# One engine for the fourth sorted pair, a gate before the next loads, two unread products fewer, and expert 0's w2 in two transfers

## The chip, the cores and the metric

The kernel runs on one core of a Trainium2 chip. The metric is the device time of one execution in microseconds (us). In the profile, PE is TensorE (products), PEld its weight loads, DVE is VectorE, ACT is ScalarE, POOL is GpSimd and SP is SyncE. POOL and SP also issue DMA transfers. Times inside an execution are counted from the start of its span.

## What is computed

Two stages follow each other. The first is an attention with sorted blocks: for 4 batches and 8 heads, a sequence of 768 rows of 64 is cut into 8 blocks of 96. A small 8x8 matrix per head is normalised five times by rows and columns and then mixes the blocks of keys and of values:

```python
k_sorted = np.einsum('bhij,bhjcd->bhicd', P, k_b)
v_sorted = np.einsum('bhij,bhjcd->bhicd', P, v_b)
scores = scale * np.matmul(q_b, k_sb.transpose(0, 1, 2, 4, 3))
out = np.matmul(softmax(scores), v_sb)
```

The second stage is a mixture of 8 experts over the resulting 3072 rows of 512: routing weights from a gate, normalised eight times, and for each expert `relu(x @ w1[e]) @ w2[e]` with w1 of 512x1024 and w2 of 1024x512, summed with the routing weights.

## The kernel before

The work is one long program for the five engines. What each engine does is in the order of its queue; most products and all POOL transfers are pinned to the order in which the program was written (`pin`), the other instructions are placed by the framework's scheduler, which also sets all semaphores. The first 38 us hold batch 0 and the start of batch 1. From 38 to about 92 us the attention of batches 1 to 3 is woven with expert 0's products for the batches already done, and then experts 1 to 7 follow for the rest of the time.

**Loads.** All loads from memory that convert to bf16 are issued by POOL, in this order (lines 91 to 97, then 476, 477 and 501, 502): q, v and k of batch 0 in halves of four heads; the gate's weights; the first half of expert 0's w1 (512 KB); later, after the hop of batch 0, the second half of w1 (`load_w1`, L82), v of batch 1 (`load_batch`, L72), the product R for batch 1 (`build_r`, L135, two POOL multiplications), k and two q loads of batch 1, and w2 of expert 0 (`load_w2`, L88, one transfer of 1024 KB). v and k of batch 2 come behind that; q of batch 2 waits for a free buffer.

**Sorting the values of batch 0** (`sort_pair`, L267 to 279, called for the four pairs of heads hp = 0 to 3). Two products (L271) fill a PSUM pair, and one engine copies it into the tile `vs`: ACT for pairs 0 and 2, DVE for pair 1. Pair 3 is shared: DVE copies the first head, ACT the second.

**The hop** (`hop`, L148 to 153). The sorted values must change partitions, so eight transfers of 97.5 KB move `vs` to `vsb`, one for each block: pieces 0, 2, 4, 6 are issued by SP and 1, 3, 5, 7 by POOL.

**Keys, scores, mixes.** `wide_keys` (L294 to 306, "k") makes the sorted keys of a pair of heads; ACT copies those of pair 0 and DVE those of pairs 1 to 3. `half_scores` (L308 to 322, "s") does four of the eight blocks for one pair of heads and ACT takes the exponential. `half_mix` (L328 to 343, "m") multiplies by the sorted values that the hop brought: m00 to m03 read pieces 0 to 3, m10 to m13 pieces 4 to 7. `half_turn` ("t") transposes the result, `half_hidden` ("h") does expert 0's first product (h02 and h03 read the second half of w1), and "v" sorts the values of batch 1 with `sort_pair`. "p" spreads the 8x8 matrices for R. `output0` (L398 to 407) reads w2 in its eight parts, the first four in a first step.

**Unread products** (`warm`, L324 to 326) are products of a blank tile that nobody reads. A table says how many stand ahead of a step. The order of all of this is written out by hand in lines 471 to 503:

```python
unread = {"s03": 1, "s10": 1, "s11": 1, "s12": 1, "m00": 3, "m02": 1, "m03": 1,
          "m10": 1, "m11": 1}
for x in ("s00 k2 s01 k3 p s02 s03 s10 s11 s12 m00 s13 m01 m02 m03 t00 m10 m11 t01 h00 "
          "m12 m13 h01 t10 h02 v0 t11 v1 h03 v2 v3 h10").split():
```

Of two digits the first is the half of the blocks (for "h" and "t" too) and the second the pair of heads or the group; one digit is the pair of heads. The PSUM pairs have four buffers, so a step also waits until the copy of an earlier step has freed one.

Of the kernel before, what the change touches and what calls it, by code (L numbers as in the profile page):

```python
# [20 lines left out]
def mkap(t, dims, off=0):  # L21
    return bass.AP(tensor=t.tensor, offset=t.offset + off, ap=dims)
# [3 lines left out]
def kernel(  # L26
# [11 lines left out]
    nc = tc.nc  # L38
    B, H, S, D = 4, 8, 768, 64
    NB, BL = 8, 96  # L40
    N, Dm, E, F = 3072, 512, 8, 1024
# [22 lines left out]
    pin = tc.keep_in_program_order  # L64
    kt, vt, qt = {}, {}, {}

    def load_batch(bb, parts):
        for x, l0, n in parts:
            d, src = {"v": (vt, v), "k": (kt, k), "q": (qt, q)}[x]
            if bb not in d:  # L70
                d[bb] = kvp.tile([128, 8, 384], BF16, name="kvq", bufs=5)
            pin(nc.gpsimd.dma_start(  # L72
                out=d[bb][:, l0:l0 + n, :],
                in_=src[bb, l0:l0 + n].rearrange("h (p kk) d -> p h (kk d)", kk=6)))

    w1t = {}
    w2t = {}

    def load_w1(e, f0=0, f1=F):
        if e not in w1t:  # L80
            w1t[e] = wp.tile([128, 4, F], BF16, name="w1e")
        pin(nc.gpsimd.dma_start(  # L82
            out=w1t[e][:, :, f0:f1],
            in_=moe_w1[e].rearrange("(kk k) f -> k kk f", k=128)[:, :, f0:f1]))

    def load_w2(e):
        w2t[e] = (wq if e else wcp).tile([128, 8, Dm], BF16, name="w2e")
        pin(nc.gpsimd.dma_start(out=w2t[e],  # L88
                                in_=moe_w2[e].rearrange("(fb k) f -> k fb f", k=128)))

    load_batch(0, [("q", l0, 4) for l0 in (0, 4)])
    Ibig = ones.tile([128, 128], BF16)
# [11 lines left out]
    VW = NB * 520  # L104
    vsbt = [perp.tile([128, VW], BF16, name=f"vsb{n}") for n in range(2)]
    vs = vsp.tile([128, 6, 8, 65], BF16)
# [145 lines left out]
    held = pp.tile([96, 2], BF16)  # L252
# [14 lines left out]
    def sort_pair(bb, hp, pair):  # L267
        t = pair()
        warm(t, bb == 0 and hp == 0)
        for h in range(2):  # L270
            pin(nc.tensor.matmul(t[:, h, 0:384], Rt[bb][:, 2 * hp + h].rearrange("p i c -> p (i c)"),  # L271
                                 vt[bb][:, 2 * hp + h, :], start=True, stop=True))
        shared = bb == 0 and hp == 3
        for eng, h0, h1 in (((nc.vector.tensor_copy, 0, 1), (nc.scalar.copy, 1, 2)) if shared else
                            ((nc.vector.tensor_copy if hp % 2 else nc.scalar.copy, 0, 2),)):
            ins = eng(vs[:, :, 2 * hp + h0:2 * hp + h1, 0:64],
                      t[:, h0:h1, 0:384].rearrange("p h (kk d) -> p kk h d", d=64))
            if shared:
                pin(ins)

    def wide_queries(hp, pair):
        qT[0, hp] = sp.tile([128, 128, 6], BF16, name="qTs", bufs=4)
        t = pair()
        for kk in range(6):
            for h in range(2):
                c = (kk % 3) * 128
                pin(nc.tensor.matmul(t[64 * h:64 * h + 64, kk // 3, c:c + 128],
                                     qt[0][:, 2 * hp + h, kk * 64:kk * 64 + 64], Ibig,
                                     start=True, stop=True))
        pin(nc.scalar.copy(  # L290
            qT[0, hp].rearrange("p x (b j) -> p x b j", b=2),
            t[:, :, 0:384].rearrange("p b (j x) -> p x b j", j=3)))

    def wide_keys(hp, pair):  # L294
        kT[0, hp] = sp.tile([128, NB, 16, 6], BF16, name="kTs", bufs=4)
        t = pair()
        for kk in range(6):
            for h in range(2):
                c = (kk % 3) * 128
                pin(nc.tensor.matmul(t[64 * h:64 * h + 64, kk // 3, c:c + 128],  # L300
                                     kt[0][:, 2 * hp + h, kk * 64:kk * 64 + 64],
                                     Rt[0][:, 2 * hp + h].rearrange("p i c -> p (i c)"),
                                     start=True, stop=True))
        pin((nc.vector.tensor_copy if hp else nc.scalar.copy)(
            kT[0, hp].rearrange("p i c (b j) -> p (i c) b j", b=2),
            t[:, :, 0:384].rearrange("p b (j x) -> p x b j", j=3)))
# [17 lines left out]
    def warm(t, n):  # L324
        for _ in range(n):
            pin(nc.tensor.matmul(t[:, 0, :], blank[:, 0:128], blank, start=True, stop=True))
# [102 lines left out]
    with tc.tile_pool(name="ps0", bufs=4, space=bass.MemoryType.PSUM,  # L429
                      reuse_waits="tile") as ps0:  # L430
        pair = lambda: ps0.tile([128, 2, 512], F32, name="pair")
        warm(pair(), 11)
        rs = pp.tile([32, 8], F32)
        cs = pp.tile([32, 8], F32)
        Pt = P.rearrange("p i j -> p j i")
        nc.vector.reduce_max(out=rs, in_=P, axis=AX.X)
        nc.vector.tensor_sub(P, P, mkap(rs, [rs.ap[0], rs.ap[1], [0, 8]]))
        for it in range(5):


            pin(nc.scalar.activation(out=P, in_=P, func=AF.Exp))
            if it == 3:
                warm(pair(), 3)
            for hp in {2: (0, 1), 3: (2,), 4: (3,)}.get(it, ()):
                wide_queries(hp, pair)
            if it == 1:
                pin(nc.vector.reduce_sum(out=mask16, in_=Ibig.rearrange("p (j c) -> p c j", c=16),
                                         axis=AX.X))
            pin(nc.vector.reduce_sum(out=rs, in_=P, axis=AX.X))
            nc.vector.reciprocal(out=rs, in_=rs)  # L450
            nc.vector.tensor_mul(P, P, mkap(rs, [rs.ap[0], rs.ap[1], [0, 8]]))
            nc.vector.reduce_sum(out=cs, in_=Pt, axis=AX.X)
            if it == 0:
                nc.vector.tensor_scalar_add(cs, cs, 1e-9)
            nc.vector.reciprocal(out=cs, in_=cs)
            nc.vector.tensor_mul(Pt, Pt, mkap(cs, [cs.ap[0], cs.ap[1], [0, 8]]))

        Prep = perp.tile([32, 8, 8, 16], BF16, name="R1")
        for eng, i0, n in ((nc.vector.tensor_copy, 0, 5), (nc.scalar.copy, 5, 3)):
            eng(Prep[:, i0:i0 + n], mkap(P, [P.ap[0], [8, n], [1, 8], [0, 16]], off=i0 * 8))  # L460

        def spread(n):
            t = pair()
            warm(t, n)
            pbps = t[:, 0, 0:256].rearrange("p (i g) -> p i g", i=8)
            for i in range(8):
                pin(nc.tensor.matmul(pbps[:, i, :], Prep[:, i].rearrange("p j c -> p (j c)"),
                                     Ibig[0:32, 0:32], start=True, stop=True))
            return pbps

        build_r(0, nc.vector, 2, spread(13))
        for hp in range(4):
            sort_pair(0, hp, pair)
        wide_keys(0, pair)
        hop(0)
        load_w1(0, 512, F)
        load_batch(1, [("v", 0, 8)])
        wide_keys(1, pair)
        halves = [mps.tile([128, 8, 384], BF16, name="hTs") for _ in range(2)]
        unread = {"s03": 1, "s10": 1, "s11": 1, "s12": 1, "m00": 3, "m02": 1, "m03": 1,  # L480
                  "m10": 1, "m11": 1}
        for x in ("s00 k2 s01 k3 p s02 s03 s10 s11 s12 m00 s13 m01 m02 m03 t00 m10 m11 t01 h00 "
                  "m12 m13 h01 t10 h02 v0 t11 v1 h03 v2 v3 h10").split():
            n = [int(c) for c in x[1:]]
            if x[0] == "s":
                half_scores(*n, pair, unread.get(x, 0))
            elif x[0] == "m":
                half_mix(*n, pair, unread.get(x, 0))
            elif x[0] == "t":
                half_turn(*n, lambda: ps0.tile([128, 2048], BF16, name="pair"),  # L490
                          nc.vector.tensor_copy if x == "t11" else nc.scalar.copy)
            elif x[0] == "h":
                half_hidden(*n, halves[n[0]], pair)
            elif x[0] == "v":
                sort_pair(1, *n, pair)
            elif x[0] == "k":
                wide_keys(*n, pair)
            else:
                nc.vector.tensor_copy(Pb, spread(0).rearrange("p i g -> p g i"))
                build_r(1, nc.gpsimd, 4)  # L500
                load_batch(1, [("k", 0, 8), ("q", 0, 4), ("q", 4, 4)])
                load_w2(0)
        hop(1)
# [323 lines left out]
    for n in range(1, 3 * (E - 1) + 1):  # L827
        e, p, hT = 1 + (n - 1) // 3, (n - 1) % 3, hTs[n - 1]
        d = 2 + n // 3
# [49 lines left out]
```

## Time and profile before

| what | value |
|---|---|
| median of 3 runs | 676.18 us (675.96 to 676.72) |
| the profiled execution | 677.16 us |
| its span, first to last instruction | 675.2 us |
| granted TensorE clock | 1.000 |
| DMA packets | 32671, 36.57 MB, mean 54 GB/s |
| PE busy, 24 to 26 us / 26 to 28 us / 28 to 30 us | 2.00 / 0.65 / 1.77 of 2 us |
| DMA, 20 to 22 / 22 to 24 / 28 to 30 / 34 to 36 us | 178 / 136 / 201 / 203 GB/s |
| POOL idle before its q load at 37.27 us | 9.6 us |

The span is what the profile's rows cover; the profiled execution's own time is 1.96 us longer. A row of the timeline gives the start, the length, the engine, the line of the program, the operation, what it writes and reads, and how many instructions are merged in it; a bracket at its end tells how long the engine was idle before it and what ended that wait. A row of the waits gives who waited for whom, the total, how often, and the longest. A DMA row gives the transfer, the queue that issued it, how many, the size of each, and the median time from issue to landing.

### The profile page before, as it was taken

The page shows a single profiled execution, that of the slowest core. Times are in us where ns is not written, and L with a number is a line of the kernel's source. Part 1 is how long each engine was busy: PE and PEld are TensorE (multiplying, and loading weights), DVE is VectorE, ACT ScalarE, POOL GpSimd, SP SyncE. Part 2 cuts the span into 40 slices and gives each one's busy share as a digit, 9 for nine tenths or more (in the row PEclk, how much of TensorE's full clock was granted, in tenths as well). Part 3 has the DMA queues.
Part 4 walks back from the last instruction along what each step waited for, and adds up shares of the span by engine and source line. Part 5 has one row for each costly group of instructions (what it writes and reads, how often), then busy time and mean ns, then how long its engine had stood idle before and what let it go on. Part 6 is the DMA issues. An engine that isn't in the chain of part 4 may idle for free.

```text
span 675.2 us, 13291 instructions
## 1 busy us (share of the span) xinstructions
PE 661.3 (98%) x5155; PEld 435.8 (65%) x5155; DVE 544.0 (81%) x1135; ACT 295.7 (44%) x530; POOL 470.2 (70%) x494
## 2 busy tenths in 40 slices
PE   7899999999999999999999999999999999999996
PEld 3666676554666666666666666666666666666675
DVE  6548777663798888888898888888898888888896
ACT  4673863479433333333434343333434343333430
POOL 4612445007987998898897998689886999636745
PEclk9999999999999999999999999999999999999999
DMA  9997964002140340031203040034003120001223
GB/s 158 184 220 121 151 113 64 1 0 40 24 64 2 63 62 1 1 63 17 48 1 62 2 64 1 2 62 63 1 1 64 19 46 1 1 1 63 94 78 142
DMA packets 32671, 36.57 MB, mean 54 GB/s; under 512 B 2016, under 2 KB 25696, under 8 KB 32608
## 3 DMA queue, kind: packets, MB, share of 16 engines
q0 software_dynamic: 26720, 27.42, 25.9%
q1 hardware_dynamic: 5888, 8.30, 3.7%
q8 instruction: 40, 0.66, 0.4%
q14 instruction: 23, 0.19, 0.1%
HBM read 52.45 MB, written 6.29 MB: 87 GB/s over the span
## 4 chain that ended last, share of the span: by engine, by line
PE 73%; DVE 1%; POOL 1%; issue 0%; ACT 0%; DVEq 0%
PE oacc L736 36%; PE bk L649 36%; PE bk L736 1%; DVE osbl L701 1%; POOL hs L719 1%; DVE hT L685 0%; DVE hT L688 0%; ACT p L669 0%; DVEq L701 0%
## 5 line engine op out<-in xcount | busy, mean ns | idle before, releaser
L701 DVE SCALAR_TENSOR_TENSOR osbl<-oacc,glog,osbl 128x256 f32<-128x256 f32 (+1 forms) x490 | 255.3, 521 | 61.5 <-PE oacc L736 61.3
L649 PE MATMUL bk<-xtT,w1e 128*128 128x512 bf16 x504 | 149.7, 379 | 0.0
L719 POOL TENSOR_TENSOR hs<-hT 128x512 bf16<-128x512 bf16 (+2 forms) x105 | 99.4, 959 | 67.8 <-DVE hT L688 67.6
L736 PEld LDWEIGHTS <-hs 128*128 128x128 bf16 x1008 | 98.5, 98 | 64.7 <-POOL hs L719 1.5
L736 PEld LDWEIGHTS <-hT 128*128 128x128 bf16 x1008 | 98.6, 98 | 64.5 <-issue 1.3
L736 PE MATMUL oacc<-w2e,hT 128*128 128x256 bf16 x796 | 119.6, 273 | 0.5 <-ACT hT L691 0.5
L691 ACT ACTIVATE hT<-bk 128x512 bf16<-128x512 f32 x84 | 50.3, 598 | 158.5 <-PE bk L649 156.5
L719 POOL TENSOR_TENSOR hs<-hT,hs 128x512 bf16<-128x512 bf16 (+2 forms) x105 | 99.8, 958 | 4.9
L719 POOL TENSOR_TENSOR hs<-hs,hT 128x512 bf16<-128x512 bf16 (+2 forms) x105 | 99.9, 959 | 4.3 <-ACT hT L691 0.4
L649 PE MATMUL bk<-xc,wc 128*128 128x512 bf16 x336 | 99.9, 379 | 0.2 <-ACT p L669 0.2
L736 PE MATMUL oacc<-w2e,hs 128*128 128x256 bf16 x612 | 92.0, 273 | 0.9 <-POOL hs L719 0.9
L677 ACT COPY u<-bk 128x512 f32<-128x512 f32 x84 | 49.2, 586 | 95.2 <-PE bk L649 94.5
L649 PEld LDWEIGHTS <-w1e 128*128 128x128 bf16 x672 | 65.7, 98 | 10.5
L685 DVE CUSTOM_DVE_ANT_0 hT<-bk,p 128x512 bf16<-128x512 f32 x84 | 58.1, 692 | 11.8 <-ACT p L682 6.4
L695 DVE SCALAR_TENSOR_TENSOR h<-bk,hT 128x512 bf16<-128x512 f32 x84 | 57.2, 681 | 5.8 <-ACT hT L691 5.8
L682 ACT COPY p<-bk 128x512 f32<-128x512 f32 x84 | 49.3, 586 | 23.5 <-PE bk L649 23.5
L669 ACT COPY p<-bk 128x512 f32<-128x512 f32 x84 | 49.3, 587 | 20.3 <-PE bk L649 20.3
L673 DVE CUSTOM_DVE_ANT_0 hT<-bk,p 128x512 bf16<-128x512 f32 x84 | 57.1, 680 | 1.1 <-ACT hT L395 0.6
L688 DVE CUSTOM_DVE_ANT_0 hT<-bk,u 128x512 bf16<-128x512 f32 x84 | 57.1, 679 | 1.0 <-PE bk L649 1.0
L736 PE MATMUL oacc<-w2s,hs 128*128 128x256 bf16 x364 | 54.8, 273 | 0.1
L649 PEld LDWEIGHTS <-wc 128*128 128x128 bf16 x504 | 49.3, 98 | 8.0 <-issue 0.4
L649 PE MATMUL bk<-xtT,wc 128*128 128x512 bf16 x168 | 50.0, 379 | 0.0
(141 smaller groups left out, 838.1 us busy)
## 6 DMA issues: line engine op xcount, KB each, us to landing
w2e<-in_moe_w_dram POOLq DMA_DIRECT2D x8, 1024.0 KB, 8.8
w1e<-in_moe_w_dram POOLq DMA_DIRECT2D x7, 1024.0 KB, 8.1
out_dram<-osbl SPq DMA_DIRECT2D x23, 256.0 KB, 2.0
kvq<-in_v_dram POOLq DMA_DIRECT2D x3, 768.0 KB, 13.1
kvq<-in_k_dram POOLq DMA_DIRECT2D x3, 768.0 KB, 14.0
vsb<-vs SPq DMA_DIRECT2D x20, 97.5 KB, 5.4
kvq<-in_q_dram POOLq DMA_DIRECT2D x4, 384.0 KB, 10.5
kvq<-in_q_dram POOLq DMA_DIRECT2D x2, 768.0 KB, 18.3
```

The source lines that it names most:

```text
L649: hold(nc.tensor.matmul(ps, wa[:, kk, :], xa[:, kk, :], start=(first and kk == 0), stop=(kk == 1), skip_group_check=True))
L669: nc.scalar.copy(p1, u)
L673: nc.vector._custom_dve(TENSOR_ADD_SAT, out=c11, in0=w, in1=p1, s0=TOP, s1=0.0)
L677: nc.scalar.copy(u2, u)
L682: nc.scalar.copy(p5, v)
L685: nc.vector._custom_dve(TENSOR_ADD_SAT, out=c22, in0=u, in1=p5, s0=TOP, s1=0.0)
L688: nc.vector._custom_dve(TENSOR_ADD_SAT, out=c12, in0=v, in1=u2, s0=TOP, s1=0.0)
L691: nc.scalar.activation(out=c21, in_=u, func=AF.Relu)
L695: nc.vector.scalar_tensor_tensor(out=h3[e, p][:, i, :], in0=u, scalar=0.0, in1=c22, op0=ALU.max, op1=ALU.subtract)
L701: nc.vector.scalar_tensor_tensor(out=o, in0=ps, scalar=glog[:, t, e:e + 1], in1=o, op0=ALU.mult, op1=ALU.add)
L719: nc.gpsimd.tensor_tensor(out=c, in0=a, in1=b, op=o)
L736: nc.tensor.matmul(ps, h[:, fb, :], w[:, fb, :], start=(first and fb == 0), stop=(fb == 3), skip_group_check=True)
```

## The change

The shared copy of pair 3 becomes a DVE copy of both heads, as for pair 1, and is no longer pinned. A POOL copy of two columns of `vsb`, the last elements of pieces 0 and 2, is placed behind the hop; the second half of w1 and v of batch 1 are issued behind that copy, and so is all that POOL does later. One unread product each goes from s12 and from m00. The w2 of expert 0 is loaded by two transfers, parts 0 to 3 and 4 to 7; the other experts' w2 stay one transfer.

```diff
     def load_w2(e):
         w2t[e] = (wq if e else wcp).tile([128, 8, Dm], BF16, name="w2e")
-        pin(nc.gpsimd.dma_start(out=w2t[e],
-                                in_=moe_w2[e].rearrange("(fb k) f -> k fb f", k=128)))
+        for f0, f1 in ((0, 8),) if e else ((0, 4), (4, 8)):
+            pin(nc.gpsimd.dma_start(
+                out=w2t[e][:, f0:f1],
+                in_=moe_w2[e].rearrange("(fb k) f -> k fb f", k=128)[:, f0:f1]))
...
-        shared = bb == 0 and hp == 3
-        for eng, h0, h1 in (((nc.vector.tensor_copy, 0, 1), (nc.scalar.copy, 1, 2)) if shared else
-                            ((nc.vector.tensor_copy if hp % 2 else nc.scalar.copy, 0, 2),)):
-            ins = eng(vs[:, :, 2 * hp + h0:2 * hp + h1, 0:64],
-                      t[:, h0:h1, 0:384].rearrange("p h (kk d) -> p kk h d", d=64))
-            if shared:
-                pin(ins)
+        (nc.vector.tensor_copy if hp % 2 else nc.scalar.copy)(
+            vs[:, :, 2 * hp:2 * hp + 2, 0:64],
+            t[:, :, 0:384].rearrange("p h (kk d) -> p kk h d", d=64))
...
         hop(0)
-        load_w1(0, 512, F)
-        load_batch(1, [("v", 0, 8)])
+        gate = nc.gpsimd.tensor_copy(
+            held, mkap(vsbt[0], [[VW, 96], [1040, 2]], off=519))
+        with tc.issue_after(gate.ins):
+            load_w1(0, 512, F)
+            load_batch(1, [("v", 0, 8)])
         wide_keys(1, pair)
         halves = [mps.tile([128, 8, 384], BF16, name="hTs") for _ in range(2)]
-        unread = {"s03": 1, "s10": 1, "s11": 1, "s12": 1, "m00": 3, "m02": 1, "m03": 1,
+        unread = {"s03": 1, "s10": 1, "s11": 1, "m00": 2, "m02": 1, "m03": 1,
                   "m10": 1, "m11": 1}
```

## The prediction

> **What bounds the kernel now.** I read the summary of engines first, then the chain that ended last, then the waits of the first 40 us, and last the timelines of each engine and the DMA issues of that stretch one by one, because everything that the change touches lies between 14 and 50 us of the span.
>
> ```profile
> PE 661.3 (98%) x5155; PEld 435.8 (65%) x5155; DVE 544.0 (81%) x1135; ACT 295.7 (44%) x530; POOL 470.2 (70%) x494
> PE 73%; DVE 1%; POOL 1%; issue 0%; ACT 0%; DVEq 0%
> ```
>
> TensorE works or is queued nearly all the time and carries the chain, so time is won only where TensorE stands still or does work that nobody reads. The waits between 12 and 40 us name the places:
>
> ```profile
> engine line waited for: us in total, times, longest us
> ...
> PE pair L335 <- DMA vsb<-vs: 1.4, 1, 1.4
> ...
> PE pair L315 <- ACT kTs L304: 0.9, 1, 0.9
> ...
> ACT vs L276 <- DVE vs L276: 0.3, 1, 0.3
> ```
>
> TensorE waits once for a hop transfer and once for the first key copy on ACT, and ACT itself waits for DVE inside the shared copy. The ACT timeline shows the second (start, us, engine, line):
>
> ```profile
> 14.22 1.51 ACT L276 CAST vs<-pair 128x768 bf16<-128x768 f32 x2 [1.44 <-PE pair L271]
> 16.01 0.50 ACT L276 CAST vs<-pair 128x384 bf16<-128x384 f32 x1 [0.28 <-DVE vs L276]
> 16.40 0.80 ACT L304 CAST kTs<-pair 128x768 bf16<-128x768 f32 x1
> ```
>
> ACT is done with pairs 0 and 2 at 15.73, waits for DVE's half of pair 3, copies its own half, and only then the first keys. TensorE's timeline shows the first:
>
> ```profile
> 22.21 0.82 PE L326 MATMUL pair<-blank 128*128 128x512 bf16 x3
> 22.87 0.51 PE L335 MATMUL pair<-vsb,atp 96*96 96x65 bf16 x8
> ...
> 25.69 0.33 PE L335 MATMUL pair<-vsb,atp 96*96 96x65 bf16 x4
> 27.37 0.33 PE L335 MATMUL pair<-vsb,atp 96*96 96x65 bf16 x4 [1.35 <-DMA vsb<-vs]
> ```
>
> The mix m00 runs at 22.87 behind three unread products and waits for nothing; m10 does its blocks 4 and 5 at 25.69 and then stands idle from 26.02 to 27.37 for piece 6. POOL and the DMA issues (of 19.5 to 20 us; last column: us to landing) show what shares the DMA engines with that piece:
>
> ```profile
> 16.80 2.11 POOL L151 DMA_DIRECT2D vsb<-vs  x4 [8.88 <-ACT vs L276]
> 18.88 0.82 POOL L82 DMA_DIRECT2D w1e<-in_moe_w_dram  x1
> 19.66 0.94 POOL L72 DMA_DIRECT2D kvq<-in_v_dram  x1
> ```
>
> ```profile
> kvq<-in_v_dram POOLq DMA_DIRECT2D x1, 768.0 KB, 13.1
> w1e<-in_moe_w_dram POOLq DMA_DIRECT2D x1, 512.0 KB, 10.0
> vsb<-vs SPq DMA_DIRECT2D x1, 97.5 KB, 8.3
> ```
>
> SP's pieces 0, 2, 4, 6 go out at 16.54, 17.27, 17.90 and 19.07 and take 3.7, 4.8, 5.9 and 8.3 us: they land at 20.2, 22.1, 23.8 and 27.4. POOL's pieces 1, 3, 5, 7 land at 20.1, 21.1, 21.8 and 22.6. The hop of batch 3 (85.8 to 93.1 us), with no load beside it, takes 3.2, 3.7, 4.6 and 5.3 us for the same four SP pieces. So the loads issued at 18.88 and 19.66 are the likely cause of piece 6's extra 3 us.
>
> **Fourth pair by one engine.** DVE's half (0.547) becomes a whole copy (0.954 in its own rows). DVE is free of pair 1 at 15.43 and then ends pair 3 at 16.39, where ACT ended the shared copy at 16.51: the hop starts 0.12 earlier. DVE's next copy, the keys of pair 1, needs products that end at 16.32 and starts at 16.40 instead of 16.35. ACT skips its wait and its half: its key copy starts when the products are done, 15.75 instead of 16.40, minus 0.65. The scores s00 follow at 16.60 (17.25), k2 at 16.91 (17.56). From there the key copies on DVE set the pace: pair 1 ends 17.35, pair 2 runs 17.50 to 18.41, pair 3 18.41 to 19.32, so s03 starts at 19.37 instead of 20.01. I take minus 0.64. The exponentials on ACT shift as much and stay ahead of their mixes.
>
> **Fewer unread products.** s12 loses one and m00 one. The timeline has 13 of them in 2.98 us, and from 21.58 to 21.90 one costs 0.21 net of overlap: minus 0.43. They kept TensorE busy in a time in which it would have waited, so this counts only if what follows is ready: m00 at 22.87 - 0.64 - 0.43 = 21.80 needs pieces 0 to 3. They landed by 22.1; the earlier start and no load beside them put the last at 21.0 to 22.0. If they stay at 22.1 - 0.12, the loss is 0.2.
>
> **The gate.** A POOL copy of 96x2 that waits for pieces 0 and 2. The trace has a copy of that form at L814: 0.17 us; 0.10 (POOL's memset of 128x1) and 1.0 (its copies of 128x768 at L179) bound it, and I take 0.17, the same shape. Behind it on POOL stand the second half of w1 (18.88), v of batch 1 (19.66), the two R products (20.57), k, q, q, w2 and v, k of batch 2 (22.59 to 27.66). The gate opens when piece 2 lands: at best 17.15 + 3.7 = 20.9 (the hop of batch 3), at worst 22.0; I take 21.2, so the loads begin at 21.5, 2.6 later than now. What it gives: no load runs beside the last pieces. At the pace of the unloaded hop of batch 2 (first issue 62.66, last landing 70.4, 7.7 us) piece 6 lands at 24.2, and m10 asks for it at 27.37 - 1.35 - 1.07 = 24.95. The stall of 1.35 goes. The bounds are 1.35 and nothing (piece 6 as late as now); a loss is excluded, since no transfer is added beside that piece.
>
> What it costs: the loads are queued in order, 203 GB/s when full. A 1024 KB w1 load alone takes 8.1 us, of which 5.2 is transfer at 203 GB/s, so 512 KB takes 5.5: landing 27.0 (28.9 now), needed by h02 at 30.1. v of batch 1 follows 3.9 later, at 30.9; by the row of batch 3's v (7.5 us alone, 3.6 above its transfer) at 31.5. Now it lands at 19.66 + 13.1 = 32.8 and is read at 33.79; with 2.42 gained it is wanted at 31.37. That is what is late next: between 0 and 0.15 lost at 31.5, up to 1.0 if the gate opens at 22.0. I take 0.15.
>
> The R products end at 25.4 and are read at 31.4. k of batch 1 lands 3.9 after v, at 35.1, wanted at 36.5. q, w2, v, k, q follow in a full queue about 1.5 earlier than now while TensorE is 2.3 earlier; their present slacks (k 2.2, first q 3.9, w2 1.7, v of batch 2 some 6, its q 4.8 through the copies on POOL) cover 0.8.
>
> [...]
>
> **w2 in two transfers.** One more issue: two of 0.79 (the row of a 512 KB w1 half) for one of 0.92, plus 0.66 on POOL, hidden in POOL's idle 9.6 us before 37.27; without that cover the loads behind would be 0.66 later. Bounds 0.6 (384 KB issues, 0.75) to 0.9. The first half lands some 2.6 earlier, but w2 as a whole lands now at 47.4 and is read at 49.1; shifted, it is about 45.9 against 46.8. I cost it at nothing; at most it saves a wait should the loads come later than I think.
>
> **The sum.** 0.64 + 0.43 + 1.35 = 2.42, minus 0.15: 2.27. After 38 us the program is the same, and TensorE's waits between 60 and 160 us are all for work that itself follows TensorE, none over 0.5 at a time, so the gain stays to the end. The profiled execution took 677.16 (span 675.2 and 1.96 around it), 0.98 above the median of the runs; it would take 674.9. On the median of 676.18: **673.9**.
>
> **Rivals.** "Same" means within 0.2% (1.35 us), about what a measurement of this kernel can tell from no change.
> - *The loads become the bound* (0.17): the gate opens at 22 or the loads still meet pieces 4 to 7, v lands at 32.2 to 32.9 and TensorE waits before the batch-1 sort. For: v's margin now is only 1.0 and its issue is 2.6 later. Against: nothing else is left in the queue then. Gain 0.8 to 1.6, about 675.0.
> - *The hop is slow by itself* (0.08): piece 6 lands at 26 because its issue is slow (SP's third issue took 1.13, the fourth starts at 19.07; 0.73 and 64.8 - 62.66 = 2.1 after the first in batch 2) and the first w1 half is still moving until 19.7. Gain 27.37 - 26 = 1.4: 674.8.
> - *Given back later* (0.07): the second hop's last piece lands at 50.2, just as its mix runs (50.03 to 50.96), and its transfers run among loads that shift less than TensorE; a wait there takes the gain: 676.2.
> - *Slower, by a late gate* (0.05): v lands some 9.9 after the gate opens. From 24 on there is no gain; each us above adds one. If piece 2 were as late as piece 6 is now (27.4), v would land at 37.3 and the sort wait 3.5: 679.7. Against: piece 2 landed at 22.1 even beside the loads.
> - *Slower, by TensorE's rate* (0.03): at the start the unread products come every 0.43 us (1.60, 2.02, 2.45), later every 0.21, though the granted clock reads 1.00 throughout. If m00 to t01 (21.8 to 25.7) ran at the first pace for want of products, that adds 3.9: 677.8. Against: after the 1.35 us pause the products at 27.53 and 27.75 still run at the fast pace. [...]
>
> The forecast has 0.60, its own range 673.2 to 674.6. Faster than 674.83: the 0.60 and 0.10 of the first two rivals' 0.25, so 0.70; same: their other 0.15 and the third's 0.07, so 0.22; slower: the last two, 0.08. The range is 673.2 to 675.9: below it lies only a hop and loads faster than every row, above it the last three rivals, 0.15.
>
> **What would show it.** Right: ACT's key copy near 15.75, s03 near 19.4, m00 near 21.8 without a DMA wait, no wait of L335 at m10, the w1 half issued near 21.5, v's products near 31.4, and logits (38.10 now) near 35.8. Wrong: a DMA wait of L271 above 0.5 us, a DMA wait at L335, ACT's key copy still after 16.3, a DMA wait between 45 and 55 us, or the gate standing anywhere on POOL but between the hop's last issue and the w1 half.

## The result, and the profile after

The changed kernel takes 674.97 us (median of 22 executions, lowest 674.2) where the kernel before takes 676.46 (22, lowest 675.75). The ratio is 0.9974, with a 95% interval of 0.9963 to 0.9985: 1.8 us less, between 1.0 and 2.5 (the two medians differ by 1.5). The forecast was 2.27 us less (673.9 on a median of 676.18), with 673.2 to 675.9 as its range. One of the 22 executions of the changed kernel took 2426 us, with products two and a half to three times as long (1104 ns instead of 379 for one of 128x512), for a reason that is not known; the ratio leaves it out, without it the median is 674.94, and the profile here is that of another execution of the same program, of 675.38 us with a span of 673.6. In the changed program most line numbers are two higher or lower: the batch-1 sort is L273, the mixes are L333, the key copies L302, the later mixes L237 and expert 0's second product L400.

The chain is still TensorE's:

```profile
PE 72%; DVE 1%; issue 1%; POOL 1%; ACT 0%; DVEq 0%
```

The waits between 12 and 60 us (who waited for whom, total, times, longest) have changed places:

```profile
PE pair L273 <- DMA kvq<-in_v_dram: 0.8, 1, 0.8
...
PE bank L237 <- DMA vsb<-vs: 0.3, 1, 0.3
...
PE pair L313 <- ACT kTs L302: 0.2, 1, 0.2
```

The mix m10's wait of 1.35 us for hop piece 6 is gone and the wait for ACT's key copy has fallen from 0.9 to 0.2. In their place stand 0.8 us for v of batch 1 and 0.3 us for the second hop. TensorE's timeline tells how far the changed kernel is ahead of the kernel before at each step (its lead):

```profile
21.47 0.51 PE L333 MATMUL pair<-vsb,atp 96*96 96x65 bf16 x8
...
24.34 0.51 PE L333 MATMUL pair<-vsb,atp 96*96 96x65 bf16 x8
...
26.76 0.81 PE L359 MATMUL pair<-xtT,w1e 128*128 128x384 bf16 x4 [0.23 <-ACT xtT L351]
...
32.01 0.48 PE L273 MATMUL pair<-kvq,R 128*128 128x384 bf16 x2 [0.78 <-DMA kvq<-in_v_dram]
```

m00 starts at 21.47 instead of 22.87 and m10's eight products run in one piece at 24.34. The second half of h00 starts at 26.76 instead of 29.49, a lead of 2.73 us. At the first batch-1 sort the lead is 1.78 (32.01 instead of 33.79); at the logits of batch 0 it is 1.85 (36.25 instead of 38.10); behind the second hop's wait it is 1.45, and it stays there: the same batch's sort at 57.21 instead of 58.67, the logits of batch 1 at 63.98 instead of 65.43. The span is 1.6 shorter.

POOL's timeline and the two loads behind the gate (DMA issues of 21.7 and 22.6 us, last column: us to landing):

```profile
21.21 0.18 POOL L474 COPY held<-vsb 96x2 bf16<-96x2 bf16 x1 [2.04 <-DMA vsb<-vs]
21.70 0.79 POOL L82 DMA_DIRECT2D w1e<-in_moe_w_dram  x1 [0.30 <-issue]
22.47 0.91 POOL L72 DMA_DIRECT2D kvq<-in_v_dram  x1
```

```profile
w1e<-in_moe_w_dram POOLq DMA_DIRECT2D x1, 512.0 KB, 6.3
...
kvq<-in_v_dram POOLq DMA_DIRECT2D x1, 768.0 KB, 9.4
```

The gate's copy starts at 21.2, v is issued 2.8 us later than before, and lands at 22.5 + 9.4 = 31.9 instead of 32.7: earlier, though not as early as it is now wanted.

### The profile page after: what moved, and what is told of

Read it like the earlier page. It is cut to its first block, busy times and chain, and to the rows that moved or that the text cites. A ratio compares the mean times of both kernels' runs of the same rounds, so it can differ in the third digit from the quotient of the medians.

```text
span 2424.2 us, 13289 instructions
## 1 busy us (share of the span) xinstructions
PE 2419.2 (100%) x5153; PEld 1001.2 (41%) x5153; DVE 594.7 (25%) x1135; ACT 303.1 (13%) x529; POOL 470.3 (19%) x496
## 4 chain that ended last, share of the span: by engine, by line
PE 100%; DVE 0%; issue 0%
PE bk L650 40%; PE oacc L737 39%; PE bank L400 3%; PE oacc L400 3%; PE bk L391 3%; PE bank L391 2%; PE pair L324 1%; PE bk L737 1%; PE bank L237 1%; PE pair L359 1%; PE bank L219 1%; PE bank L248 1%; PE bank L198 1%; PE pair L273 0%; PE bank L160 0%; PE bank L185 0%
## 5 line engine op out<-in xcount | busy, mean ns | idle before, releaser
L650 PE MATMUL bk<-xtT,w1e 128*128 128x512 bf16 x504 | 485.1, 1104 | 0.0
L737 PEld LDWEIGHTS <-hs 128*128 128x128 bf16 x1008 | 223.5, 222 | 387.5 <-issue 369.1
L737 PEld LDWEIGHTS <-hT 128*128 128x128 bf16 x1008 | 223.5, 222 | 386.8 <-issue 386.8
L737 PE MATMUL oacc<-w2e,hT 128*128 128x256 bf16 x796 | 383.1, 693 | 0.0
L650 PE MATMUL bk<-xc,wc 128*128 128x512 bf16 x336 | 323.3, 1104 | 0.0
L737 PE MATMUL oacc<-w2e,hs 128*128 128x256 bf16 x612 | 294.5, 692 | 0.0
L737 PE MATMUL oacc<-w2s,hs 128*128 128x256 bf16 x364 | 175.3, 694 | 0.0
L650 PE MATMUL bk<-xc,w1e 128*128 128x512 bf16 x168 | 161.8, 1105 | 0.0
L650 PE MATMUL bk<-xtT,wc 128*128 128x512 bf16 x168 | 161.3, 1101 | 0.0
L737 PE MATMUL oacc<-w2s,h 128*128 128x256 bf16 x184 | 88.6, 697 | 0.0
```

Of the source, the lines that this page charges most:

```text
L650: hold(nc.tensor.matmul(ps, wa[:, kk, :], xa[:, kk, :], start=(first and kk == 0), stop=(kk == 1), skip_group_check=True))
L737: nc.tensor.matmul(ps, h[:, fb, :], w[:, fb, :], start=(first and fb == 0), stop=(fb == 3), skip_group_check=True)
```

## The experiments

All kernels of one table row group ran on one chip beside the kernel before. The last two columns split the executions by their mean granted TensorE clock: how many stood below 0.998, and the median of the others. One stretch of 3.4 us at half clock, as the profiles below show it, lowers the mean of an execution of 675 us by 0.0025. Medians on different chips differ for the same program (675.38 and 674.88 for the changed one, which did not run on the second chip), so a difference of a few tenths between the groups says nothing.

| kernel | median us | ratio to before (95%) | below 0.998 | median of the others |
|---|---|---|---|---|
| before (first chip) | 677.06 | | 10 of 35 | 676.79 |
| changed, again | 675.38 | 0.9970 (0.9953 to 0.9986) | 1 of 12 | 675.38 |
| copy alone | 676.21 | 0.9985 (0.9967 to 1.0004) | 3 of 12 | 675.97 |
| gate alone | 676.49 | 0.9979 (0.9963 to 0.9996) | 1 of 12 | 676.49 |
| fewer unread alone | 678.01 | 1.0006 (0.9985 to 1.0027) | 8 of 12 | 676.50 |
| before (second chip) | 677.09 | | 10 of 35 | 676.66 |
| changed, w2 whole | 675.74 | 0.9978 (0.9965 to 0.9992) | 2 of 12 | 675.66 |
| changed, gate on piece 0 | 675.35 | 0.9964 (0.9949 to 0.9979) | 0 of 12 | 675.35 |
| changed, gate on pieces 4 and 6 | 677.04 | 0.9996 (0.9982 to 1.0011) | 5 of 12 | 676.59 |
| changed, unread as before | 674.79 | 0.9962 (0.9949 to 0.9975) | 0 of 12 | 674.79 |
| before (third chip) | 676.70 | | 6 of 28 | 676.61 |
| changed, third time | 674.88 | 0.9969 (0.9954 to 0.9983) | 0 of 11 | 674.88 |
| changed, no gate | 677.13 | 1.0002 (0.9985 to 1.0019) | 6 of 12 | 675.75 |
| changed, h03 first | 674.66 | 0.9966 (0.9951 to 0.9980) | 0 of 7 | 674.66 |
| h03 first, unread as before | 674.89 | 0.9968 (0.9957 to 0.9980) | 0 of 11 | 674.89 |

**The changed kernel again**, without an edit, twice.

> The changed kernel itself, for a profile and a time beside the others. Theory (the sum of the prediction): s03 starts near 19.4 us, m00 near 21.8, no wait of L333's products for a hop transfer, the w1 half issued near 21.5, the batch-1 sort near 31.4 with a wait for v under 0.2; 2.3 us less than before. Rival 1 (the loads become the bound): a DMA wait of 0.5 to 1.0 us at the first batch-1 sort, 0.8 to 1.6 us less than before. Rival 2 (the hop is slow by itself): a hop wait of 0.5 to 1.0 us left at m00 or m10.

> The changed kernel once more, beside the three that follow on the same chip. All theories: 1.5 to 2.0 us less than before, a wait for v of batch 1 between 0.5 and 1.7 at the sort and a wait of up to 0.4 for the second hop.

The profile above is that of the first. No mix waits for the first hop, as the theory has it, so rival 2 falls; m00 comes at 21.47, earlier than the 21.8 of the theory. The wait for v is 0.78 in the first and 0.53 in the other (the sort at 32.01 and 31.67), which is the wait of rival 1; the medians are 1.7 and 1.8 us below the kernel before, a little more than that rival allowed.

**The copy alone** (`sort_pair` as in the change, the rest as before):

```diff
-        shared = bb == 0 and hp == 3
...
+        (nc.vector.tensor_copy if hp % 2 else nc.scalar.copy)(
```

> Only the fourth pair's copy goes to one engine. Theory: ACT's first key copy starts near 15.75 instead of 16.40 and the scores 0.6 earlier, but m10 waits for piece 6 anyway, which lands only 0.1 earlier: the wait at m10 grows from 1.35 to about 1.9 and the time falls by 0.1 us (0 to 0.2). Rival: the scores' lead is kept past m10 because the hop pieces come earlier by as much: 0.5 us less.

The front leads by 0.82 at m00 (22.05 instead of 22.87) and all of it goes into the wait for piece 6:

```profile
27.55 0.33 PE L331 MATMUL pair<-vsb,atp 96*96 96x65 bf16 x4 [2.35 <-DMA vsb<-vs]
```

In this execution (677.07) nothing is gained, as the theory says. The median of the executions is lower than it says, 0.8 us below the kernel before, with an interval that just includes no change. The landing of piece 6 moves between executions (26.6 to 27.5 in the four profiles without a gate), so one profile can't settle whether the earlier hop brings it in earlier; that stays open.

**The gate alone:**

```diff
+        gate = nc.gpsimd.tensor_copy(
+            held, mkap(vsbt[0], [[VW, 96], [1040, 2]], off=519))
+        with tc.issue_after(gate.ins):
+            load_w1(0, 512, F)
+            load_batch(1, [("v", 0, 8)])
```

> Only the gate: the second half of w1 and v of batch 1 wait for hop pieces 0 and 2. Theory: piece 6 lands near 24.5 instead of 27.4, m10 (wanted at 26.0) does not wait, v lands near 31.5 and is wanted at 32.4: 1.35 us less than before. Rival 1 (the loads become the bound): v lands at 32.5 or later and the sort waits: 1.2 us less or smaller. Rival 2 (the hop is slow by itself): m10 still waits 0.5 us or more: 0.8 us less at most.

m10 no longer waits, and the logits of batch 0 come at 36.74 instead of 38.10, the gain of the theory (1.36). v lands in time. But most of the gain is lost at a place that no theory named, the first product with w2:

```profile
48.81 0.39 PE L402 MATMUL bank<-w2e,hTs 128*128 128x512 bf16 x1 [1.04 <-DMA w2e<-in_moe_w_dram]
```

w2 as one transfer is issued at 28.87 behind the gate and takes 19.9 us: it lands at 48.8, where the lead wants it at 47.8. The granted clock falls right behind that wait (windows of 4 us; the third column from the right is the clock):

```profile
44.00:48.00 4.00, 3.60 (x73) 2.43 (x72) 1.05 (x2) 4.00 (x12) 0.00 (x0) 1.00 1.20 241
48.00:52.00 4.00, 3.00 (x21) 2.05 (x23) 1.08 (x6) 2.35 (x6) 0.00 (x0) 0.64 1.31 205
...
49.15:52.50 3.35, 3.16 (x22) 2.05 (x21) 1.58 (x8) 1.20 (x4) 0.00 (x0) 0.50 1.31 203
```

The last line, a narrower window, shows that the clock does not stand at 0.64: it is half from 49.1 to 52.5 us and full on both sides.

This profiled execution (678.66) is the slowest of its kernel; the other eleven have a mean clock of 0.999 or more. Their median is 0.3 below that of the kernel before in the last column, about what a gain of 1.36 and a wait of 1.04 leave.

**Fewer unread products alone** (one less at s12 and m00).

> Only the two unread products go. Theory: m00 starts 0.4 us earlier and m10 waits 0.4 longer for piece 6, nothing else moves: 0.0 us (within 0.1). Rival (TensorE's rate falls for want of products): products after m10 come at twice the distance for a stretch, 1 us or more slower.

m00 starts at 22.14, 0.7 earlier, and m10 waits 1.47. Where the clock holds the time is 676.5, 0.3 below the kernel before, which the runs do not separate from nothing. But 8 of 12 executions stand below 0.998, with a median of 678.35, where the kernel before has 10 of 35. So in these runs the clock fell more often with the two products gone and TensorE still waiting for piece 6. The profiled execution is not one of the eight (its clock is 1.000), so where in the program the clock falls in them is not shown, nor that the rival's place, behind m10, is the one.

**w2 whole again**, the rest as changed:

> The changed kernel with w2 of expert 0 in one transfer again. The prediction's theory (the split is worth nothing): the time of the changed kernel, within 0.2 us, no DMA wait at L400's products. Theory from the first runs (the split covers a later queue): w2 as a whole lands near 47.8 us, as its second half does in the changed kernel, and is wanted at 47.2; a DMA wait of 0.5 to 0.7 at the first w2 product, of which 0.3 to 0.4 falls on the wait for the second hop that follows: 0.2 to 0.6 us slower than the changed kernel, 1.0 to 1.4 less than before.

The median is 0.4 to 0.9 us above those of the changed kernel, but on another chip, and the ratios to the kernel before (0.9978 here, 0.9970 and 0.9969 there) have intervals that overlap widely: what the split is worth in time is not shown. In the profile w2 lands at 27.64 + 20.7 = 48.3 and the first w2 product waits 0.16 for it at 48.36, though v had already held TensorE 1.74 in that execution. With the lead of the changed kernel's profile, whose first w2 product runs at 47.31 and whose second half of w2 lands at 47.7, w2 as a whole would have cost a wait of about 0.4 there (an estimate from these two numbers).

**The gate on piece 0, and on pieces 4 and 6:**

```diff
-            held, mkap(vsbt[0], [[VW, 96], [1040, 2]], off=519))
+            held, mkap(vsbt[0], [[VW, 96], [1, 2]], off=518))       # piece 0
...
+            held, mkap(vsbt[0], [[VW, 96], [1040, 2]], off=2599))   # pieces 4, 6
```

> The changed kernel with a gate that reads two columns of piece 0 alone. Theory (v of batch 1 is the bound, and it lands 10.4 us after the gate's copy): piece 0 lands 0.8 to 1.0 earlier than piece 2, so the loads start near 20.8 and v lands near 31.0; its wait of 0.8 goes, m10 still does not wait (piece 6 near 23.5, wanted at 24.5): 0.8 us less than the changed kernel, of which up to 0.4 may go again in a longer wait for the second hop. Rival (the loads then meet the last pieces): a hop wait at m10 and v no earlier than now: no gain.

> The changed kernel with a gate that reads pieces 4 and 6. Theory (the late-gate rival of the prediction, each us of gate is a us of v): the gate opens near 23.5 instead of 21.2, v lands near 34.1 and the sort waits 3.0 instead of 0.8: 2.2 us slower than the changed kernel, 0.5 slower than before. Rival (once the hop is out of the way the loads run faster and make it up): v lands before 33, 1 us slower than the changed kernel or less.

The first sort, with piece 0 as the gate and with pieces 4 and 6, and the two loads of each:

```profile
32.84 0.48 PE L273 MATMUL pair<-kvq,R 128*128 128x384 bf16 x2 [1.65 <-DMA kvq<-in_v_dram]
```

```profile
w1e<-in_moe_w_dram POOLq DMA_DIRECT2D x1, 512.0 KB, 8.5
...
kvq<-in_v_dram POOLq DMA_DIRECT2D x1, 768.0 KB, 11.5
```

```profile
33.24 0.48 PE L273 MATMUL pair<-kvq,R 128*128 128x384 bf16 x2 [2.13 <-DMA kvq<-in_v_dram]
```

```profile
w1e<-in_moe_w_dram POOLq DMA_DIRECT2D x1, 512.0 KB, 5.5
...
kvq<-in_v_dram POOLq DMA_DIRECT2D x1, 768.0 KB, 8.7
```

The two loads issued at 20.39 and 21.17 land no earlier than those of the changed kernel: the w1 half takes 8.5 us and v lands at 32.7. Those issued at 23.66 and 24.44 take 5.5 and 8.7, and v lands at 33.1, only 1.2 later than in the changed kernel for a gate 2.0 later. The rival of the first expectation held in part: m10 did not wait, but v came no earlier. One profile does not settle that the overlap with the last pieces is why, since with the change's own gate v landed anywhere from 31.0 to 32.8 in six profiles, and 32.7 lies inside that. All nine profiles with a gate, taken together, speak for it: the w1 half takes 5.5 us where piece 6 lands at most 0.3 after its issue (the late gate, the gate alone), 5.5 to 6.3 where it lands 1.4 to 1.7 after (five profiles), 7.5 at 2.0 (w2 whole) and 8.5 at 3.0 (piece 0), and v lands 3.8 to 4.1 behind it in all nine. No run changes the overlap alone. What stands is the time: the early gate equals the changed kernel. The late one loses the whole gain, 1.7 to 2.2 us by the medians against the changed kernel on the two other chips; the theory had said 2.2, the rival at most 1. Part of that is the clock, which stands below 0.998 in 5 of its 12 executions: in the last column the loss is 1.2 to 1.7. Behind the wait of 2.13 the clock is half from 34.4 to 37.8 us.

**Unread products as before**, the rest as changed:

> The changed kernel with the unread products of before. Theory (the front has a lead that v's landing takes): m00 is 0.7 later, v lands at the same 31.9 and the sort's wait falls from 0.8 to 0.1: the same time as the changed kernel within 0.15 us. The prediction's sum (0.43 of path for the two products): 0.4 us slower.

v is wanted later and is there, no wait is shown at the sort, and it starts earlier than in the changed kernel's first profile:

```profile
31.75 0.48 PE L273 MATMUL pair<-kvq,R 128*128 128x384 bf16 x2
```

The time is not above that of the changed kernel (674.79, beside 675.38 and 674.88 on other chips). With v as the bound, no gain of the two products fewer is shown.

**No gate**, the rest as changed:

> The changed kernel without its gate (copy, fewer unread products, w2 in two transfers). Theory (the gate is what lets the front's lead through): m00 near 21.5, then a wait of 2.7 us at m10 for piece 6, which lands near 27.4; 0.2 us less than before (0 to 0.4). Rival (the copy and the unread products bring the gain, the gate only moves the wait to v): 1.2 us less than before or better.

```profile
26.68 0.33 PE L333 MATMUL pair<-vsb,atp 96*96 96x65 bf16 x4 [2.15 <-DMA vsb<-vs]
...
27.75 2.49 PE L359 MATMUL pair<-xtT,w1e 128*128 128x384 bf16 x8
30.03 1.46 PE L333 MATMUL pair<-vsb,atp 96*96 96x65 bf16 x16
```

m10 waits 2.15 us, and what follows runs slower: eight L359 products take 2.49 (two groups of 0.82 and 0.81 with 0.23 between them before) and sixteen L333 products 1.46 instead of 0.87, at a granted clock that is half from 28.1 to 31.5 us. The logits come at 38.63, later than before, although piece 6 landed earlier than in the profile of before. The median is not below that of before. Where the clock held, 6 of 12 executions, it is 675.75, 0.9 less than before and more than the theory allowed, as with the copy alone (0.8 in that column); why is open. Beside the changed kernel on the same chip the gate is worth 2.2 us, or 0.9 where the clock held. No run has the change without the copy, so what the copy adds to the gate is read from the timelines alone.

**h03 ahead of the sorts**, with the change's products and with those of before:

```diff
-                  "m12 m13 h01 t10 h02 v0 t11 v1 h03 v2 v3 h10").split():
+                  "m12 m13 h01 t10 h02 t11 h03 v0 v1 v2 v3 h10").split():
```

> The changed kernel with t11 and h03 moved ahead of the four sorts of batch 1 in the written order, so that v is wanted 1.6 us later. Theory (v's landing is what eats the lead): v is wanted at 32.7 and lands at 31.6 to 32.8, the wait of 0.8 goes, logits start near 35.5 instead of 36.25; 0.7 us less than the changed kernel, of which up to 0.3 may come back as a longer wait for the second hop. Rival (the second hop takes whatever is won): no less than the changed kernel.

> As h03_first, with the unread products of before. Theory (with v out of the way the products that nobody reads are on the path again): 0.65 us slower than h03_first, about the changed kernel's time. Rival (the lead of the front is lost anyway, to v or to the second hop): the same time as h03_first within 0.2.

The wait for v is gone, and that for the second hop too (its first piece is issued at 35.22, instead of 35.85 in the changed kernel's profile on the same chip):

```profile
32.47 1.55 PE L273 MATMUL pair<-kvq,R 128*128 128x384 bf16 x8
35.52 0.74 PE L263 MATMUL bank<-wg,xtT 128*128 128x8 bf16 x24
```

The logits come 0.4 earlier than in that profile (35.91), and the batch-1 logits 0.75 earlier (62.91 instead of 63.66). The medians differ by only 0.2 (674.66 and 674.88) and their intervals overlap, so that this order is better than the change is not shown. With the unread products of before its profile is 0.8 later at the logits, and its median 0.2 higher: the direction of the theory, a third of its size, not separable.

## Why the prediction was right or wrong

**The bound, right.** TensorE's wait for piece 6 and its wait behind ACT's copy were what could be won: the first went, the second fell from 0.94 to 0.22.

**The fourth pair, right.** ACT's key copy starts at 15.67 (15.75 forecast), s00 at 16.52 (16.60), s03 at 19.27 (19.37), a lead of 0.74 where the sum had 0.64.

**The unread products, mis-sized.** I took 0.43 for the two on the path, from their own pace of 0.21. From s03 to m00 it is 2.20 instead of 2.86, so they were worth 0.66: in the kernel with only this edit, s11, m00's first unread product and m00 start at 21.21, 21.70 and 22.14 where it was 21.27, 22.21 and 22.87, which is 0.45 for the product ahead of s12 and 0.22 for the one ahead of m00. Why the first is worth twice its pace is open. With 0.10 more from the copy, the lead at h00 is 2.73 instead of 2.42. But in the time that term was not worth what the sum gave it: with v as the bound no gain is left of it, as the kernel with the old products shows.

**The gate, right in what it gives** (no wait at m10, opening at 21.2 as taken, 1.36 on the logits when alone). The loads begin at 21.70, 0.2 later than the 21.5 of the forecast, since 0.30 pass between the copy and the first issue.

**The loads behind it, the step that failed in size.** "I take 0.15" for v's wait: the changed kernel showed 0.78 and 0.53, and the variants with w2 whole and with the gate on piece 0 showed 1.74 and 1.65. I had timed the w1 half as a load alone, 5.5 us. Behind this gate it took 6.3, with four pieces still to land, the last of them (piece 6) 1.7 after its issue, while the two kernels whose gate opened as the last piece landed showed 5.5. v lands 3.9 behind it, as forecast: at 31.9 instead of 30.9 to 31.5. And v was wanted at 31.06, 0.3 earlier than I had it. The wait of the rival "the loads become the bound", which had a chance of 0.17, is what happened, though v landed earlier than its 32.2 to 32.9; its gain of 0.8 to 1.6 holds the 1.5 of the medians and misses the 1.8 of the ratio.

**"I cost it at nothing"**, the w2 split: the size is open, the reason was wrong. I had the queue about 1.5 earlier up to w2, at 45.9. In the changed kernel v and k land 0.8 earlier than before and the q loads 0.6, and the second half of w2 lands at 28.5 + 19.2 = 47.7, later than the whole did before (47.4); the first half lands at 43.6. The second hop, issued 1.9 earlier than before, probably takes part of the queue's room there, which no run separates. So w2 as a whole would have come after its first product at 47.31. The gate without the split waits 1.04 for it.

**"Given back later", right in part.** The second hop's wait took 0.3 of the 1.85 that were left, 0.4 with the restart.

**The sum.** 2.73 at h00, minus 0.95 at v (the wait of 0.78 and the restart behind it), plus 0.07, minus 0.40 at the second hop: 1.45 at 57 us, where the prediction had 2.27. The end of the span is 1.6 earlier. So the direction and the mechanism are right, and the gain on the timeline is two thirds of the forecast: a front 0.31 better than forecast, against 0.8 more at v and 0.4 at the second hop. The median of 674.97 lies outside the forecast's own 673.2 to 674.6 and inside the range only because that made room for the rivals, and two of the forecast's signs of being wrong came up (a wait for v above 0.5 us, a DMA wait between 45 and 55 us).

**TensorE's rate, wrong in sign for this change.** I gave it 0.03 as a way to lose. The runs show it the other way: of the kernel before 26 of the 98 executions beside the experiments stand below a mean clock of 0.998, and the medians of those three groups of executions are 2.1 to 3.3 us above the others; of the changed kernel's 23 executions one does. That the shorter waits are the reason is my guess and not shown, since no execution of the kernel before with a lower clock was profiled. In the "others" column, free of it, the change brings 1.4 and 1.7 us. And "the granted clock reads 1.00 throughout" misread the start: in the trace of the kernel before the first clock record begins at 6.51 us; ahead of it there is no record, and the column then shows 1.00. The unread products that start every 0.43 us, the last of them at 5.44, all stand ahead of that record; three behind it, from 7.18, take 0.82 us together. What clock was granted at the start is not shown, and so neither is the reason for the slow pace there.

## What to carry to other kernels

When a wait goes, price the next transfer that the earlier work will ask for, in the queue that the change itself makes, and not from a row of that transfer alone: here the lead of 2.7 us met v and then the second hop, and with w2 in one transfer w2 as well, and each took a part. Where a gate opens has to be weighed on both sides: no gate lost the gain, one that opened 1.3 us earlier gave the same time, and one that opened 2.0 later lost all again. And work that fills a wait was not free to remove here while the wait was still there: without it TensorE's mean clock stood below 0.998 in 8 of 12 executions, where the kernel before has 10 of 35.

## What the runs showed of the hardware

In three profiles a single wait of TensorE of 1.0 to 2.2 us was followed by one stretch of 3.4 us at half the granted clock (from 28.1 us without the gate, from 49.1 with the gate alone, from 34.4 with the late gate). Eight L359 products that lie for the most part in such a stretch took 2.49 us without the gate and 2.57 with the late gate, where eight behind it take 1.47 in the same two profiles. In three other profiles no such stretch followed, with waits of 2.35 us (the copy alone), 1.74 (w2 whole) and 1.65 (the gate on piece 0): the clock reads 1.00 there in every window from 20 to 60 us.

So the length of a wait alone does not tell here whether the clock falls: it fell behind 1.04 us with the gate alone and held behind 2.35 with the copy alone. What decides is not shown.

The loads behind the hop gave single landings that do not follow the issue: v of batch 1 landed at 32.7, 32.7, 31.9 and 33.1 us when the w1 half ahead of it was issued at 18.9, 20.4, 21.7 and 23.7. The third of these varies from 31.0 to 32.8 between profiles, so that only so much is shown: an issue up to 2.8 us earlier brought no landing ahead of that band.
